# A delta-rule attention and a routed mixture of experts on one core: one sort product a chunk, narrower state and w products, earlier masks, two idle products

## The chip, the cores and the metric

The kernel runs on one core of one Trainium2 chip. The metric is device time in microseconds of one execution; before the change the median of three runs is 519.18 us (518.67 to 519.23). A further execution was taken with the hardware profiler; all lines of traces below come from it. Names of engines in its lines: PE is TensorE (PEld its weight loads), DVE is VectorE, ACT is ScalarE, POOL is GpSimd, SPq the queue of SyncE, which issues the DMAs.

## The reference

Two blocks, one after the other, in float32:

```python
# attention: batch 4, heads 8, 768 positions, head size 48
for t in range(S):
    y[:, :, t] = q[:, :, t] @ state                       # per batch and head
    v_old = state^T k_n[:, :, t]                          # k_n = k / (|k| + 1e-6)
    state += beta_t * outer(k_n[:, :, t], v_t - v_old)
x = y.transpose(0, 2, 1, 3).reshape(3072, 384)
# experts: 4 groups of 4, hidden size 1024
g_idx = argmax(x @ w_group); e_idx = argmax(x @ w_expert[g_idx])
out[token] = softmax_g * softmax_e * (relu(x @ w1[g, e]) @ w2[g, e])
```

Each of the 3072 tokens goes to one of 16 experts.

## The kernel before

**Attention in chunks.** The 768 positions are cut into 24 chunks (`NCH`) of 32 (`C`). The partitions hold 4 batches times 32 positions; a "quad" is the 32 partitions of one batch, a "pair" 64 partitions of two. Within a chunk the recurrence becomes a triangular system. `gram` (L251) makes the products of keys with keys and queries with keys; ScalarE copies them out (`gt`, `gq`). `inverse(g)` solves the triangular systems of four chunks at once (a group; six groups, `RG` = 4) on VectorE by about 95 small operations (L279 to L377), and transposes the result into `mt`. `spread` (L386, L388) copies `mt` into `mtb`, once for each parity of the batch and multiplied by 0 or 1 (`parity`), so that a 64x64 weight block for two batches has zeros off its diagonal. `mask(u)` (L268) does the same for the query products of chunk u, with the causal mask (`upper`), into `gqm`. `scale(u)` (L403) makes `vh`, the values of chunk u times the key norms.

**One chunk on TensorE.** `advance(u)` has four steps: (1) `a_ps` = `vh` (L416, an identity product) plus keys times state `s_bd` (L422), copied with the sign turned to `f` (ScalarE, L426), and queries times state into `o_ps` (L431); (2) `w_ps` = inverse times `f` (L439, by pairs), copied to `w` (L442); (3) the state product `s_ps` += keys times `w` (L449), its diagonal blocks copied to `s_bd` by ScalarE in two instructions (L455); (4) `o_ps` += masked queries times `w`, by pairs while later grams are made (L463), by quads in the last `LEAD` = 10 chunks (L468), copied to `x` (L472). Each product is recorded as two load and two matmul records.

**Routing and sorting.** `logits(u)` turns `x` round (L490), multiplies it by the router weights (L500). `route(r)` works for a group of four chunks (the last four chunks are two groups of two): choices, the place of each token within its expert (`place`), the weight (`what`), and per chunk a selection matrix `at` (L561, `turn_to`), which has a one where a token's place equals a column from 0 to 255 (`T` = 2 tiles of 128 columns). Two products per chunk (L621), one for each tile, add the tokens' row numbers and weights into `sorted_in`, which shares the first bank of `s_ps` with the state: columns 384 to 479. Groups 0 to 3 are "early" and do much of it on GpSimd; group 4 (chunks 16 to 19) and the last two on VectorE.

**The order.** All engines run in an order written out by hand (`manual_schedule`). The loop over chunks calls the steps; between them `work(n)` lets the tasks behind (an inverse, a route) issue VectorE instructions as far as their due allows (`due` grows by n * 180 times a rate, `SHARE` = 0.64 for an inverse), and `allow(...)` releases tasks held at a name. At the end of chunk u's turn come `mask(u + 1)` and `scale(u + 2)`, and then the loads of later chunks:

```python
work(12)
if u + 1 < NCH:
    mask(u + 1)
if u + 2 < NCH:
    scale(u + 2)
```

Ahead of the loop stand twelve grams, the first inverse, and the first step of chunk 0; the grams borrow the banks of `s_ps`, which is only later the state.

**Experts.** After the sort, each of the 16 experts takes up to 256 sorted tokens: `hidden` (L964), `second` (L983), weights loaded two experts ahead by SyncE's queue, tokens gathered and scattered by GpSimd.

Of the kernel before, what the change touches and what calls it, by code (L numbers as in the profile page):

```python
# [8 lines left out]
F32 = mybir.dt.float32  # L9
I32 = mybir.dt.int32  # L10
AX = mybir.AxisListType
ALU = mybir.AluOpType
# [3 lines left out]
C = 32  # L16
# [11 lines left out]
def constants(n_tokens, seq, n_experts, n_group, n_batch):  # L28
# [11 lines left out]
                                 .reshape(C, 2 * C) for b in range(n_batch)], axis=0),  # L40
        "tiny": np.full((128, 1), 1e-36),
# [25 lines left out]
def deltanet_then_moe(  # L67
# [109 lines left out]
    with ExitStack() as first:  # L177
# [10 lines left out]
        NB, NV = LEAD + 2, 3  # L188
        kqt_ = [ap_.tile([128, 2, NP, 128], F32, name=f"kqt{i}") for i in range(NB)]
# [74 lines left out]
        def mask(u):  # L264

            like = [128, H, 2, C]
            gqs[u] = wk.tile(like, F32, tag="gqm", name=f"gqm{u}", bufs=3)
            nc.vector.tensor_tensor(  # L268
                gqs[u], raws.pop(u)[:, :, None, :].to_broadcast(like),
                cut["upper"].rearrange("p (a t) -> p a t", a=2)[:, None].to_broadcast(like),  # L270
                op=ALU.mult)

        def inverse(g):
# [104 lines left out]
            mtb = wk.tile([128, RG * H, 2, C], F32, tag="mtb", name=f"mtb{g}")  # L378
            yield C * C
            turned_over.add(g)  # L380

            def spread(uu, a):
                rows = slice(uu * H, (uu + 1) * H)
                from_, by = mt.rearrange("p i r -> p r i")[:, rows], cut["parity"][:, a:a + 1]
                if g == uu == a == 0:
                    nc.vector.tensor_scalar(mtb[:, rows, a], from_, by, None, op0=ALU.mult)  # L386
                else:
                    nc.scalar.activation(mtb[:, rows, a], from_, ACT.Copy, scale=by)  # L388

            yield ACT_STEP  # L390
            for a in range(2):
                spread(0, a)
            mts[g] = mtb
            for uu in range(1, RG):
                for a in range(2):
                    yield SPREAD
                    spread(uu, a)
# [12 lines left out]
        def advance(u):  # L410
# [26 lines left out]
            for h in range(H):  # L437
                for b in pairs:
                    nc.tensor.matmul(w_ps[b, h], lhsT=mt[b, uu * H + (h % 2) * NP + h // 2],  # L439
                                     rhs=f[b, h], start=True, stop=True, skip_group_check=True)  # L440
# [5 lines left out]
            if u < NCH - 1:  # L446
                for j in range(NP):
                    for b in range(B):
                        nc.tensor.matmul(s_at[:, b, j], lhsT=k[quads[b], j],  # L449
# [9 lines left out]
            for h in range(H):  # L459
# [6 lines left out]
                else:  # L466
                    for b in range(B):
                        nc.tensor.matmul(o_ps[quads[b], h], lhsT=gq[quads[b], hq, b % 2],  # L468
# [36 lines left out]
        def route(r):  # L505
# [50 lines left out]
            mine = small("mine", [3, NE])  # L556
            like = [128, n, 3, NE]
            def turn_to(u):
# [3 lines left out]
                    at.rearrange("p t i -> p (t i)"), cut["places"], place[:, u:u + 1], None,  # L562
# [35 lines left out]
            if not final:  # L598
                nc.vector.tensor_reduce(place[:, u0:u0 + n], rk, axis=AX.X, op=ALU.add)
                yield  # L600
            nc.vector.reciprocal(what[:, u0:u0 + n, 2:3], cw)
            yield
            cs = slice(2 if not early and final else 0, 3)
            like[2] = cs.stop - cs.start
            (nc.gpsimd if early else nc.vector).tensor_tensor(
                mine[:, :, cs], hotf[:, :, None, :].to_broadcast(like),
                what[:, u0:u0 + n, cs, None].to_broadcast(like), op=ALU.mult)
# [5 lines left out]
            for g, u in enumerate(us):  # L613
# [5 lines left out]
                yield SORT  # L619
                for t in range(T):  # L620
# [65 lines left out]
        with tc.manual_schedule(engines={mybir.EngineType.PE, mybir.EngineType.DVE,  # L686
# [23 lines left out]
            for u in range(2 * RG, LEAD):  # L710
                gram(u, homes[u % len(homes)])
            start(inverse(1), 0.95)
# [55 lines left out]
            for u in range(NCH + 1):  # L768
# [3 lines left out]
                turned = logits(u - 1) if u else iter([None] * 2)  # L772
                if u:
# [55 lines left out]
                if u + 1 < NCH:  # L829
                    mask(u + 1)  # L830
# [366 lines left out]
```

## Time and profile before

| | us |
|---|---|
| median of three runs | 519.18 |
| the profiled execution | 511.25 |
| its span, first to last instruction | 509.0 |
| TensorE busy, of the span | 470.6 |
| VectorE busy | 250.3 |
| ScalarE busy | 188.9 |
| GpSimd busy | 193.7 |
| first w product starts | 42.49 |
| last w product (chunk 23) starts | 225.33 |
| first expert product starts | 238.95 |

The span is cut into stages: up to 42 us the first inverse, to 238 us the chunks with routing behind them, then the experts. A line of the chain of waits says when a piece of work began, how long it held the chain, and the engine, tile and line. A line of the timeline has start, duration, engine, line, operation, output and inputs, shapes. A record count behind x counts half products, as each is recorded twice.

### The profile page before, as it was taken

To read this page: it belongs to the slowest core of one execution; us is meant where nothing else is said; L and a number is where in the kernel's file an instruction comes from. 1 tells how busy PE (TensorE), PEld (TensorE's weight loads), DVE (VectorE), ACT (ScalarE), POOL (GpSimd) and SP (SyncE) were. 2 spreads that over 40 slices of the span, in tenths; PEclk is the share of its full clock that TensorE was granted. 3 is DMA by queue.
4 is the path that set the end of the run, shared out by engine and by line. 5 is a ranking of instruction groups with operands and counts; after the bars stand their busy time and mean duration, and the time that the engine had idled before them with its cause. 6 is when DMAs were issued, how large, how long until landed. Compare 5 with 4: busy or idle time off the path is not lost.

```text
span 509.0 us, 18246 instructions
## 1 busy us (share of the span) xinstructions
PE 470.6 (92%) x7844; PEld 437.8 (86%) x7844; DVE 250.3 (49%) x829; ACT 188.9 (37%) x397; POOL 193.7 (38%) x288
## 2 busy tenths in 40 slices
PE   4346999999999999999999999999999999999993
PEld 3235878888888888889999999999999999999992
DVE  3999999999999995527312012102201121011110
ACT  3224768687676767652111111111111211111110
POOL 0040200633806425010445564466435654355231
PEclk9999999999999999999999999999999999999997
DMA  5781434444423546210798788769868978879740
GB/s 178 246 311 40 153 135 157 160 154 158 134 71 117 160 147 198 74 45 17 180 370 249 250 268 269 228 220 331 269 193 282 321 270 260 262 253 310 256 134 26
DMA packets 57333, 99.94 MB, mean 196 GB/s; under 512 B 18974, under 2 KB 41433, under 8 KB 57251
## 3 DMA queue, kind: packets, MB, share of 16 engines
q1 hardware_dynamic: 51331, 88.76, 52.7%
q0 software_dynamic: 5920, 10.00, 6.4%
q8 instruction: 63, 1.03, 0.8%
q14 instruction: 19, 0.16, 0.1%
HBM read 84.61 MB, written 14.27 MB: 194 GB/s over the span
## 4 chain that ended last, share of the span: by engine, by line
PE 57%; DMA 20%; DVE 7%; ACT 5%; SPq 4%; issue 4%; POOL 2%; DVEq 0%; POOLq 0%; ACTq 0%
PE y_ps L983 12%; PE h_ps L964 12%; DMA y_dram<-yq 9%; DMA out_dram<-yo,to_i 5%; PE w_ps L439 5%; PE s_ps L449 5%; DMA yr<-y_dram 5%; PE a_ps L422 3%; SPq L1023 3%; PE l_ps L500 3%; ACT s_bd L455 3%; PE o_ps L463 3%; PE o_ps L431 3%; PE g_ps L251 2%; PE a_ps L416 2%
## 5 line engine op out<-in xcount | busy, mean ns | idle before, releaser
L983 PE MATMUL y_ps<-hid,w 128*128 128x224 f32 (+15 forms) x768 | 132.2, 331 | 0.0
L983 PEld LDWEIGHTS y_ps<-hid,w 128*128 128x128 f32 x768 | 129.0, 190 | 0.3
L964 PE MATMUL h_ps<-xt,w 128*128 128x232 f32 (+14 forms) x720 | 122.7, 330 | 0.0
L964 PEld LDWEIGHTS h_ps<-xt,w 128*128 128x128 f32 x720 | 120.1, 190 | 0.3
L936 POOL DMA_INDIRECT xq<-x_dram,from_q x92 | 87.6, 952 | 36.5 <-issue 24.1
L986 DVE COPY yt<-y_ps 128x232 f32<-128x232 f32 (+13 forms) x14 | 5.1, 366 | 139.7 <-PE y_ps L983 139.7
L967 ACT ACTIVATE hid<-h_ps 128x448 f32<-128x448 f32 (+15 forms) x64 | 32.1, 502 | 100.2 <-PE h_ps L964 100.2
L995 POOL DMA_INDIRECT out_dram<-yo,to_i x32 | 34.1, 1066 | 91.5 <-DVE yo L1033 80.0
L988 ACT ACTIVATE yt<-y_ps 128x224 f32<-128x224 f32 (+15 forms) x34 | 11.5, 337 | 116.6 <-PE y_ps L983 116.6
L360 DVE TENSOR_TENSOR t<-m 128x81 f32<-128x81 f32 (+13 forms) x156 | 51.8, 332 | 0.2
L366 DVE TENSOR_TENSOR m<-m,t 128x81 f32<-128x81 f32 (+13 forms) x156 | 51.4, 330 | 0.0
L455 ACT ACTIVATE s_bd<-s_ps 48x768 f32<-48x768 f32 x46 | 37.0, 805 | 13.9 <-PE s_ps L449 13.3
L343 DVE SCALAR_TENSOR_TENSOR m<-m 128x29 f32<-128x29 f32 (+27 forms) x174 | 40.7, 237 | 0.4
L388 ACT ACTIVATE mtb<-mt,con 128x256 f32<-128x256 f32 x47 | 34.2, 741 | 1.6 <-DVE mt L377 1.5
L1033 DVE TENSOR_SCALAR yo<-yr,gate 128x384 f32<-128x384 f32 (+14 forms) x28 | 11.1, 416 | 43.0 <-DMA yr<-y_dram 35.4
L439 PE MATMUL w_ps<-f,mtb 64*64 64x48 f32 x768 | 28.0, 224 | 3.9 <-DVE mtb L386 3.9
L251 PE MATMUL g_ps<-kqt 48*32 48x64 f32 (+1 forms) x1216 | 18.5, 241 | 13.5 <-issue 8.8
L439 PEld LDWEIGHTS w_ps<-f,mtb 64*64 64x64 f32 x768 | 25.1, 138 | 6.2 <-ACT mtb L388 4.1
L422 PEld LDWEIGHTS a_ps<-s_bd,kqt 128*32 128x32 f32 x736 | 15.3, 111 | 15.5 <-ACT s_bd L455 7.3
L539 POOL TENSOR_TENSOR acc<-acc,hots 128x16 f32<-128x16 f32 x16 | 5.7, 354 | 60.1 <-DVE hots L537 59.1
L251 PEld LDWEIGHTS g_ps<-kqt 48*32 48x32 f32 x1216 | 14.6, 118 | 15.3 <-issue 10.5
L449 PE MATMUL s_ps<-w,kv 32*128 32x96 f32 x736 | 27.4, 286 | 0.1
(159 smaller groups left out, 603.5 us busy)
## 6 DMA issues: line engine op xcount, KB each, us to landing
w<-in_w_dram SPq DMA_DIRECT2D x29, 1536.0 KB
kv<-in_kv_dram SPq DMA_DIRECT2D x24, 448.0 KB, 4.1
kqt<-in_kq_dram SPq DMA_DIRECT2D x20, 512.0 KB, 4.2
x_dram<-x SPq DMA_DIRECT2D x24, 192.0 KB, 2.3
w<-in_w_dram SPq DMA_DIRECT2D x24, 128.0 KB, 3.7
y_dram<-yq SPq DMA_DIRECT2D x36, 84.0 KB, 9.2
yr<-y_dram SPq DMA_DIRECT2D x14, 192.0 KB, 2.5
kqt<-in_kq_dram SPq DMA_DIRECT2D x8, 256.0 KB, 3.5
```

The costliest lines, as they stand in the source:

```text
L251: nc.tensor.matmul(g_out[quads[b], hh * NP + j, of], lhsT=kqt[rows, 0, j, quads[b]], rhs=kqt[rows, of, j, quads[b]], start=True, stop=True ...
L343: nc.vector.scalar_tensor_tensor(row, in0=m[:, j, 0:j], scalar=m[:, i, j:j + 1], in1=row, op0=ALU.mult, op1=ALU.add)
L360: nc.vector.tensor_tensor(tv, m[:, j + 2:, j:j + 1].to_broadcast([128, n, j]), m[:, j:j + 1, 0:j].to_broadcast([128, n, j]), op=ALU.mult)
L366: nc.vector.tensor_tensor(below, below, tv, op=ALU.add)
L388: nc.scalar.activation(mtb[:, rows, a], from_, ACT.Copy, scale=by)
L439: nc.tensor.matmul(w_ps[b, h], lhsT=mt[b, uu * H + (h % 2) * NP + h // 2], rhs=f[b, h], start=True, stop=True, skip_group_check=True)
L449: nc.tensor.matmul(s_at[:, b, j], lhsT=k[quads[b], j], rhs=w[quads[b], 2 * j:2 * j + 2], start=(u == 0 and j == 0), stop=True, skip_group_ ...
L455: nc.scalar.activation(s_bd[rows, :, :, hh, :], s_at[rows, :, :, hh * D:(hh + 1) * D], ACT.Copy)
L936: nc.gpsimd.indirect_dma_start(out=xq[:, g, :], out_offset=None, in_=x_dram[:, :].rearrange("n (q c) -> (n q) c", q=4), in_offset=bass.Ind ...
L964: nc.tensor.matmul(h_ps[:, k], lhsT=w1[:, j, (f + k) * 128:(f + k + 1) * 128], rhs=xt[:, j, 0:R], start=(j == 0), stop=(j == DC - 1), skip ...
L983: nc.tensor.matmul(y_ps, lhsT=w2[:, f, j * 128:(j + 1) * 128], rhs=hid[:, f], start=(f == 0), stop=(f == FC - 1))
L995: put = nc.gpsimd.indirect_dma_start(out=out[:, :], out_offset=bass.IndirectOffsetOnAxis(ap=to[0:P, i:i + 1], axis=0), in_=yo[0:P, :], in_ ...
```

## The change

- **State product.** Keys of a pair of heads lie in 128 columns, of which the last 16 are padding; 112 columns (`KR`) are loaded, and 112 rows of `s_ps` written.
- **Sort.** For chunks 0 to 19 (`one`) `at` has 128 columns only, from the place less 128 where it is 128 or more (`low`). What tells the two tiles apart moves to the other operand: `half` is one for the tile that a token is in, `what2` is `what` times `half` for both tiles, `mine` has 96 columns in place of 48. One product with 96 columns takes the place of two with 48.
- **Late masks.** From chunk 14 (`LATE`) on `mask` writes 256 elements a partition, with a mask of its own (`causal`, 32 more columns of constants), for the quads that L468 reads.
- **Last w.** For the last group (`SMALL`, chunks 20 to 23) `spread` makes one copy in place of two, without the multiplication, and w is made by quads, 32x32.
- **Order.** `mask(u + 1)` is called at the start of chunk u's turn, not at its end (chunk 0 excepted).
- **Idle products.** Two products of the identity with 384 columns of `below` into the first bank of `s_ps`, after the last gram ahead of the loop; nobody reads their values. They begin the bank's accumulation on all 128 rows.

```diff
@@ -38,6 +38,7 @@
     out = {
         "upper": np.concatenate([np.where(np.arange(2)[None, :, None] == b % 2, (i < k)[:, None], 0)
                                  .reshape(C, 2 * C) for b in range(n_batch)], axis=0),
+        "causal": np.tile(i < k, (n_batch, 1)),
         "tiny": np.full((128, 1), 1e-36),
         "eps": np.full((128, 1), 1e-6),
         "parity": np.stack([p // C % 2 == b2 for b2 in range(2)], axis=1),
@@ -186,6 +187,7 @@
         s_ps = pst.tile([128, B, 512], F32, tag="state", name="s_ps")
         s_at = s_ps[:, :, 0:H * D].rearrange("p b (j d) -> p b j d", j=NP)
         NB, NV = LEAD + 2, 3
+        LATE, SMALL, KR = NCH - LEAD, NGR - 1, 64 + D
         kqt_ = [ap_.tile([128, 2, NP, 128], F32, name=f"kqt{i}") for i in range(NB)]
         kv_ = [ap_.tile([128, H * (64 + D)], F32, name=f"kv{i}") for i in range(NV)]
 
@@ -264,7 +266,14 @@
         def mask(u):
 
             like = [128, H, 2, C]
-            gqs[u] = wk.tile(like, F32, tag="gqm", name=f"gqm{u}", bufs=3)
+            gqm = wk.tile(like, F32, tag="gqm", name=f"gqm{u}", bufs=3)
+            if u >= LATE:
+                gqs[u] = gqm.rearrange("p h a t -> p (h a t)")[:, 0:H * C].rearrange(
+                    "p (h t) -> p h t", t=C)
+                nc.vector.tensor_tensor(gqs[u], raws.pop(u), cut["causal"][:, None, :].to_broadcast(
+                    [128, H, C]), op=ALU.mult)
+                return
+            gqs[u] = gqm
             nc.vector.tensor_tensor(
                 gqs[u], raws.pop(u)[:, :, None, :].to_broadcast(like),
                 cut["upper"].rearrange("p (a t) -> p a t", a=2)[:, None].to_broadcast(like),
@@ -376,23 +385,28 @@
             mt = wk.tile([128, C, RG * H], F32, tag="mt", name=f"mt{g}", bufs=1)
             nc.vector.transpose(out=mt.rearrange("p i r -> p (i r)"), in_=flat)
             mtb = wk.tile([128, RG * H, 2, C], F32, tag="mtb", name=f"mtb{g}")
+            one_each = mtb.rearrange("p r a t -> p (r a t)")[:, 0:RG * H * C].rearrange(
+                "p (r t) -> p r t", t=C)
             yield C * C
             turned_over.add(g)
 
             def spread(uu, a):
                 rows = slice(uu * H, (uu + 1) * H)
                 from_, by = mt.rearrange("p i r -> p r i")[:, rows], cut["parity"][:, a:a + 1]
-                if g == uu == a == 0:
+                if g >= SMALL:
+                    nc.scalar.activation(one_each[:, rows], from_, ACT.Copy)
+                elif g == uu == a == 0:
                     nc.vector.tensor_scalar(mtb[:, rows, a], from_, by, None, op0=ALU.mult)
                 else:
                     nc.scalar.activation(mtb[:, rows, a], from_, ACT.Copy, scale=by)
 
+            halves = range(1 if g >= SMALL else 2)
             yield ACT_STEP
-            for a in range(2):
+            for a in halves:
                 spread(0, a)
-            mts[g] = mtb
+            mts[g] = one_each if g >= SMALL else mtb
             for uu in range(1, RG):
-                for a in range(2):
+                for a in halves:
                     yield SPREAD
                     spread(uu, a)
 
@@ -435,7 +449,7 @@
             mt = mts[g]
             w_ps = ps.tile([128, H, D], F32, tag="s", name=f"w_ps{u}")
             for h in range(H):
-                for b in pairs:
+                for b in quads if g >= SMALL else pairs:
                     nc.tensor.matmul(w_ps[b, h], lhsT=mt[b, uu * H + (h % 2) * NP + h // 2],
                                      rhs=f[b, h], start=True, stop=True, skip_group_check=True)
             w = wk.tile([128, H, D], F32, tag="w", name=f"w{u}")
@@ -446,7 +460,7 @@
             if u < NCH - 1:
                 for j in range(NP):
                     for b in range(B):
-                        nc.tensor.matmul(s_at[:, b, j], lhsT=k[quads[b], j],
+                        nc.tensor.matmul(s_at[0:KR, b, j], lhsT=k[quads[b], j, 0:KR],
                                          rhs=w[quads[b], 2 * j:2 * j + 2],
                                          start=(u == 0 and j == 0), stop=True,
                                          skip_group_check=True)
@@ -465,7 +479,7 @@
                                          skip_group_check=True)
                 else:
                     for b in range(B):
-                        nc.tensor.matmul(o_ps[quads[b], h], lhsT=gq[quads[b], hq, b % 2],
+                        nc.tensor.matmul(o_ps[quads[b], h], lhsT=gq[quads[b], hq],
                                          rhs=w[quads[b], h], start=False, stop=True,
                                          skip_group_check=True)
             x = wk.tile([128, DM], F32, tag="x", name=f"x{u}", bufs=4)
@@ -553,13 +567,19 @@
                 nc.scalar.activation(rk, r_ps, ACT.Copy)
             nc.scalar.activation(sx, sx, ACT.Exp)
             sums, ed, cw = small("sums", [L5]), small("ed", [G]), small("cw", [1])
-            mine = small("mine", [3, NE])
+            one = u0 < near[0]
+            mine = small("mine", [T * 3 if one else 3, NE])
             like = [128, n, 3, NE]
+            if one:
+                half, low, what2 = small("half", [T]), small("low", []), small("what2", [T, 3])
+                like[2] = T * 3
             def turn_to(u):
 
                 at = wk.tile([128, T, TILE], F32, tag="at", name=f"at{u}", bufs=6)
                 (nc.gpsimd if early else nc.vector).tensor_scalar(
-                    at.rearrange("p t i -> p (t i)"), cut["places"], place[:, u:u + 1], None,
+                    at[:, 0] if one else at.rearrange("p t i -> p (t i)"),
+                    cut["places"][:, 0:TILE] if one else cut["places"],
+                    low[:, u - u0:u - u0 + 1] if one else place[:, u:u + 1], None,
                     op0=ALU.is_equal)
                 ats[u] = at
 
@@ -598,13 +618,32 @@
             if not final:
                 nc.vector.tensor_reduce(place[:, u0:u0 + n], rk, axis=AX.X, op=ALU.add)
                 yield
+            if one:
+                at_u = place[:, u0:u0 + n]
+                nc.vector.tensor_scalar(half[:, :, 0], at_u, float(TILE), None, op0=ALU.is_lt)
+                nc.vector.tensor_scalar(half[:, :, 1], at_u, float(TILE), None, op0=ALU.is_ge)
+                yield
+                nc.vector.scalar_tensor_tensor(low, in0=half[:, :, 1], scalar=-float(TILE),
+                                               in1=at_u, op0=ALU.mult, op1=ALU.add)
+                yield
             nc.vector.reciprocal(what[:, u0:u0 + n, 2:3], cw)
             yield
+            if one:
+                to_both = [128, n, T, 3]
+                (nc.gpsimd if early else nc.vector).tensor_tensor(
+                    what2, what[:, u0:u0 + n, None, :].to_broadcast(to_both),
+                    half[:, :, :, None].to_broadcast(to_both), op=ALU.mult)
             cs = slice(2 if not early and final else 0, 3)
-            like[2] = cs.stop - cs.start
-            (nc.gpsimd if early else nc.vector).tensor_tensor(
-                mine[:, :, cs], hotf[:, :, None, :].to_broadcast(like),
-                what[:, u0:u0 + n, cs, None].to_broadcast(like), op=ALU.mult)
+            if one:
+                (nc.gpsimd if early else nc.vector).tensor_tensor(
+                    mine, hotf[:, :, None, :].to_broadcast(like),
+                    what2.rearrange("p n t c -> p n (t c)")[:, :, :, None].to_broadcast(like),
+                    op=ALU.mult)
+            else:
+                like[2] = cs.stop - cs.start
+                nc.vector.tensor_tensor(
+                    mine[:, :, cs], hotf[:, :, None, :].to_broadcast(like),
+                    what[:, u0:u0 + n, cs, None].to_broadcast(like), op=ALU.mult)
             if early:
                 yield SOON
             elif not final:
@@ -617,6 +656,13 @@
                 if r < NGR - 2 and u == u0:
                     yield NEXT
                 yield SORT
+                if one:
+                    nc.tensor.matmul(sorted_in["at"], lhsT=at[:, 0],
+                                     rhs=mine[:, g].rearrange("p c e -> p (c e)"),
+                                     start=not sorted_in["begun"], stop=True,
+                                     skip_group_check=True)
+                    sorted_in["begun"] = True
+                    continue
                 for t in range(T):
                     nc.tensor.matmul(sorted_in["at"][:, t * 3 * NE:(t + 1) * 3 * NE],
                                      lhsT=at[:, t], rhs=mine[:, g].rearrange("p c e -> p (c e)"),
@@ -709,6 +755,9 @@
             next(ahead)
             for u in range(2 * RG, LEAD):
                 gram(u, homes[u % len(homes)])
+            for n in (H * D, H * D):
+                nc.tensor.matmul(s_ps[:, 0, 0:n], lhsT=ident, rhs=cut["below"][:, 0:n],
+                                 start=True, stop=True, skip_group_check=True)
             start(inverse(1), 0.95)
             made = 0
             while 0 not in mts:
@@ -770,6 +819,8 @@
                     add_gathered(gathered, [0])
                 step = advance(u) if u < NCH else iter([None] * 4)
                 turned = logits(u - 1) if u else iter([None] * 2)
+                if 0 < u < NCH - 1:
+                    mask(u + 1)
                 if u:
                     next(step)
                 else:
@@ -826,8 +877,8 @@
                 if u % RG == RG - 3 and u // RG + 2 < NGR:
                     start(inverse(u // RG + 2), SHARE)
                 work(12)
-                if u + 1 < NCH:
-                    mask(u + 1)
+                if u == 0:
+                    mask(1)
                 if u + 2 < NCH:
                     scale(u + 2)
                 if u + NB < NCH:
```

## The prediction

> **What bounds the kernel now.** I read three stages first (columns: stretch in us, its length, then busy us of each engine with its instruction count, clock, DMA share, GB/s), then the page's slices.
>
> ```profile
> 42.00:197.00 155.00, 152.01 (x4429) 129.23 (x4433) 152.71 (x546) 108.02 (x209) 54.91 (x120) 1.00 0.42 137
> 197.00:238.00 41.00, 39.66 (x958) 34.84 (x955) 17.06 (x74) 24.12 (x51) 6.29 (x7) 1.00 0.23 75
> 238.00:509.00 271.00, 262.39 (x1569) 261.11 (x1568) 47.90 (x98) 43.94 (x99) 125.89 (x141) 0.99 0.75 244
> ...
> DVE  3999999999999995527312012102201121011110
> ```
>
> From 42 to 197 us TensorE (152.0 of 155) and VectorE (152.7 of 155) are both full. After 197 VectorE is half empty, and after 238 the experts keep TensorE full. No edit touches the experts, so the gain is how much sooner the attention ends.
>
> Which of the two full engines has the last word? The chain of waits names TensorE and ScalarE. One late chunk (17) of it: start, us, what.
>
> ```profile
> 177.31 0.87 PE a_ps L422 x32
> 178.18 0.66 PE o_ps L431 x32
> 178.84 0.48 PE t_ps L490 x3
> 179.31 0.38 PE s_ps L621 x4
> 179.69 1.06 PE w_ps L439 x32
> 180.76 0.78 PE l_ps L500 x6
> 181.53 1.12 PE s_ps L449 x32
> 182.69 0.04 issue
> 182.74 0.81 ACT s_bd L455
> 183.57 0.81 ACT s_bd L455
> ```
>
> A period is 7.11 us. The sort (L621), w (L439) and state product (L449) stand on it, so what they lose the period loses, until something else arrives last. VectorE is nearly that something. The timeline shows what it owes TensorE:
>
> ```profile
> 174.48 0.54 DVE L403 TENSOR_TENSOR vh<-kv,normt 128x384 f32<-128x384 f32 x1
> 176.24 0.91 PE L416 MATMUL a_ps<-vh,con 128*128 128x384 f32 x2
> ...
> 193.79 1.25 DVE L377 STREAM_TRANSPOSE mt<-m 128x1024 f32<-128x1024 f32 x1
> 196.37 1.37 ACT L388 ACTIVATE mtb<-mt,con 128x256 f32<-128x256 f32 x2
> 197.64 1.63 ACT L455 ACTIVATE s_bd<-s_ps 48x768 f32<-48x768 f32 x2
> ```
>
> The vh of chunk 17 ends at 175.02 and is read at 176.24: 1.2 us to spare. The last inverse is transposed by 195.04, ScalarE spreads it from 196.37. In this stage VectorE idles for about 1.5 us in all, in pieces of 0.25 us at most, none of them for TensorE. Its instructions stand in a fixed order, so each has a date that a faster TensorE cannot move.
>
> **What the Trainium skill says.** "TensorE: Matmul & The Clock Gate", section "LDWEIGHTS (loading the stationary operand)": the time goes with the columns, P/1.2 ns, not the rows. The trace agrees: 128 columns 192 ns (L449), 64 columns 138 (L439), 32 columns 105 (L468); 54 ns for 64 columns is 0.84 ns a column. The same page, Part 1: an idle array runs at half clock, and about 3.4 us of sustained work release it. The trace agrees on the halves (L416 x2 takes 1.65 us at 49.91, 0.91 at 58.50) but not on the time: TensorE works from 42.49 almost without a gap and is fast only from about 52. The same page's "Architectural detail" says that VectorE and ScalarE queues are strict FIFO, which the fixed dates rest on.
>
> **The change, part by part.**
>
> *State product, 112 columns for 128.* It is bound by loads: 32 records in 1.08 us, 34 ns each, four row groups side by side. Sixteen columns less are 13 ns of a load, a quarter of that per record, 3.3 x 32 = 0.11 us; in proportion (1/8 of 1.08) 0.135. I take 0.12 a chunk, for 23 chunks. No 112-column load is in the trace: nothing gained is the lower end unless an odd width breaks the overlap (a rival below).
>
> *Sort, one product for two.* 4 records become 2 of the same load and twice the columns (96). Twelve records took 1.37 us from start to the next w (216.31 to 217.68), 0.114 each, eight 1.0, 0.12 each: 0.24 saved for each of 20 chunks. It is paid by small VectorE operations (two halves, low), five times: 128x4 operations of 0.17 us, each 0.085 to 0.2 of VectorE's time, depending on whether it waits for its forerunner: 0.3 to 0.5. In groups 1 and 2 the reciprocal waited 0.24 for GpSimd, which covers half. To chunk 19 I count 0.5 + 0.2 + 0.2 = 0.9 us.
> GpSimd: four factors (at) per group fall from 1.0 to about 0.5 each, mine doubles (0.6 to about 1.1), what2 is new (0.3 to 1.0, as cw shows). The first at of a group comes 0.1 to 1.0 later; that of group 3 is ready at 198.44 and needed at 201.1. After a shift of 1.9 us 0 to 0.8 is left. I count nothing; the other end is 0.3 us.
>
> *Late masks halved.* Spacing to the next instruction is 602 ns for 512 elements and 468 for 384 (vh): 1.05 ns an element, so 256 save 0.27. Masks 14 to 16 lie ahead of vh(17): 0.8. Ahead of the last inverse there were masks to 18, five whole ones (3.0); then masks to 19, six halves (2.0): 1.0 saved.
>
> *Masks half a period sooner.* In VectorE's order mask(u+1) goes ahead of chunk u's inverse work; it waits only for copies made ten chunks earlier and for a buffer read three chunks before. Mask(16) ended at 174.5, 0.9 us before its reader; it gets a period more. vh(u+2) has the same work ahead of it. Cost 0: without the move mask(16) would be the next wait, at a gain over 0.9.
>
> *Last w by 32x32.* 32x32 products stand in the trace: L468, 64 records in 0.81 us (212.58 to 213.39), against 1.06 for 64x64. 0.25 for each of four chunks. The spreads fall from two to one a chunk: 0.74 us of ScalarE each.
>
> *Two idle products.* Two like L416 cold, 3.3 us, from the last gram (ends 38.6) to 41.9; the first w waits for VectorE's spread until 42.46. Cover 0.5 us. If they release the clock, chunk 0 to 1 shortens: 42.49 to 53.80 is 11.3 against a warm 7.55, up to 3.7 us. From below: nothing. `causal` adds 16 KB to the first constants, under 0.1 us at the 178 GB/s of that slice.
>
> **The sum.** TensorE alone would be, at chunk 17, 16 x 0.12 + 9 x 0.24 = 4.1 us ahead (7.8 with the clock). It can't be: vh(17) is there at 175.02 - 0.8 + 0.9 = 175.1, 0.1 for the semaphore, 175.2 against 176.24: gain **1.05**. The clock's 3.7 us are therefore lost whatever happens, and the sort and state savings before chunk 17 too. Chunks 17 and 18 add 0.36 each: 1.8 at chunk 19, and 2.2 when its state product ends. There the spread of the last inverse, ahead of s_bd on ScalarE, waits for 195.04 - 1.0 + 0.9 = 194.9; one spread of 0.74 gives 195.7, against 197.64: gain **1.9**. After it VectorE is out of the way.
> Chunk 20: sort 0.24, w 0.25, of which ScalarE's second spread takes back 0.13, state 0.12: 0.48. Chunk 21: two sorts 0.48, w 0.25, state 0.12: 0.85. Chunk 22: 12 and 8 records halved 1.2, w 0.25, state 0.12: 1.58. Chunk 23: none, its w copy waits behind two ScalarE products (L742). Together **2.9**.
> 1.9 + 2.9 = 4.8 us. The profiled execution took 511.25 us (span 509.0), so it becomes 506.4; the median of the runs lies 7.9 above it, and the same 4.8 taken from 519.18 gives **514.4**. A measurement of this kernel tells about 0.2% (1 us) from no change.
>
> **Rivals.**
> *A, the sum above*, VectorE's dates decide: 513.4 to 515.4, chance 0.60.
> *B, the new small work lands on the dates:* halves and low cost 0.5 in every group (0.6 more by chunk 17), what2 and mine stall the sorts of chunk 20, the loads of 112 gain nothing. 4.8 - 0.6 - 0.3 - 0.4 = 3.5, to 1.5 if stalls repeat: 515.4 to 518. For it: 1.2 us of margin at chunk 17; GpSimd's cw takes 1.0 us for four elements. Chance 0.17.
> *C, VectorE yields:* its dates move with TensorE. Then 3.7 + 22 x 0.12 + 12 x 0.24 + 2.9 = 12.1, 507.1; halfway 511. Against it: hardly any idle time on VectorE. Chance 0.13, most of it near 512.
> *D, slower:* 112 columns are no multiple of 32, and loads of the four row groups no longer overlap. Each record is then 34 ns plus what is lost; it decides from 4.8 / (23 x 32) = 6.5 ns a record on. Without any overlap a load is spaced like L500's, 0.78 / 6 = 130 ns: 32 x 96 = 3.1 us a chunk, some 70 us slower, 585. For it: no such width in the trace; against: time goes with columns, smoothly, at 32, 64 and 128. Chance 0.06.
> *E, nothing measurable* (stalls eat all but 1 us): 0.04.
>
> **How the numbers follow.** Faster is A, B and C: 0.90; same 0.04; slower 0.06. The range takes A, B to 516.8 (0.12) and C down to 512.2 (0.08): 0.80.
>
> **What would show it.** L449's loads near 178 ns and its 32 records near 0.95 us; L621 with half the records; L439 of the last four chunks near 0.81. VectorE still full to about 196, its last mt within 0.5 us of 195.0: the decisive line. A wait of a_ps L416 for vh near chunk 17, and of the spread for mt at chunk 19, both absent before. Products near 42 us in half the time, and yet no gain from it later. Expert stage unchanged at 271 us. Wrong if mt(5) ends much sooner, if o_ps waits for gqm, or if L621 waits for at.

## The result, and the profile after

The changed kernel took 511.44 us (median of four, 510.37 to 514.39), the kernel before 518.92 (four, 517.76 to 519.23; three of the four are those that the forecast started from): a ratio of 0.9869, with a 95% interval from 0.9825 to 0.9913, that is 4.5 to 9.1 us. The forecast was 4.8 us and 514.4, with a range from 512.2; the time lies 0.8 us below that range.

Later samples, with more executions of the same two kernels, give a smaller gain:

| sample | chip | changed | before | ratio (95%) | gain, us |
|---|---|---|---|---|---|
| on record, 4 and 4 executions | not recorded | 511.44 | 518.92 | 0.9869 (0.9825 to 0.9913) | 6.8 |
| e4, 22 and 65 | 12 | 509.03 | 512.69 | 0.9939 (0.9915 to 0.9963) | 3.1 |
| e9, 15 and 50 | 0 | 510.22 | 512.59 | 0.9945 (0.9920 to 0.9969) | 2.8 |

The medians are over all executions, while the ratios, and the gains taken from them, are estimated without the few slow ones, so that they aren't the quotients of the medians. So 4.8 us lies between them, and two things need explaining: why the base moves so much, and why the better samples stop at 3.

The profiled execution of the changed kernel took 511.43 us, span 509.7. That is no less than the profiled one of before (511.25), which stood 7.9 us under the median of the timed ones. Stages and VectorE's slices, as before:

```profile
42.00:197.00 155.00, 148.59 (x4410) 123.80 (x4409) 153.12 (x559) 108.33 (x210) 51.73 (x123) 0.99 0.43 138
197.00:238.00 41.00, 38.24 (x1067) 32.80 (x1063) 16.54 (x80) 21.42 (x46) 5.59 (x8) 1.00 0.23 73
238.00:509.00 271.00, 262.08 (x1565) 260.48 (x1563) 47.90 (x98) 43.94 (x99) 126.16 (x141) 0.99 0.75 244
...
DVE  2999999999999995427212012011211121101110
```

To 197 us TensorE is now busy 148.6 us, 3.4 less, and VectorE 153.1, as full as it was. The chain of waits, the turn of chunk 17 (7.11 us before):

```profile
177.95 0.87 PE a_ps L436 x32
178.82 0.66 PE o_ps L445 x32
179.48 0.48 PE t_ps L504 x3
179.96 0.20 PE s_ps L660 x2
180.15 1.06 PE w_ps L453 x32
181.22 0.78 PE l_ps L514 x6
181.99 1.01 PE s_ps L463 x32
183.09 0.81 ACT s_bd L469
183.92 0.81 ACT s_bd L469
```

From 177.95 to the next a_ps at 184.78 it is 6.83, which is 0.28 less: the sort gave 0.18 and the state product 0.11, where the forecast had 0.36 for both. VectorE's dates in the same execution:

```profile
175.04 0.55 DVE L417 TENSOR_TENSOR vh<-kv,normt 128x384 f32<-128x384 f32 x1
176.88 0.91 PE L430 MATMUL a_ps<-vh,con 128*128 128x384 f32 x2
...
193.96 1.25 DVE L386 STREAM_TRANSPOSE mt<-m 128x1024 f32<-128x1024 f32 x1
```

The last inverse ends at 195.21 (195.04 before); the forecast was 194.9. But a_ps of chunk 17 starts 1.3 us after its vh, so it isn't this date that holds it here. One line of the waits tells of something new (waited for: us in total, times, longest), on GpSimd:

```profile
PE s_ps L660 <- POOL at L579: 2.4, 2, 1.8
```

and the timeline around the second of these waits shows what followed it:

```profile
164.75 0.46 PE L660 MATMUL s_ps<-mine,at 128*128 128x96 f32 x2 [0.66 <-POOL at L579]
...
166.98 1.82 PE L463 MATMUL s_ps<-w,kv 32*112 32x96 f32 x32
168.74 1.50 PE L482 MATMUL o_ps<-w,gqm 32*32 32x48 f32 x64
```

The last two products take 1.04 and 0.88 us elsewhere. The record of the clock has one stretch of half speed here, from 167.0 to 170.4. Later, in chunks 20 to 22, TensorE stood idle for 1.1 us that no engine explains ("issue"), 0.9 of it in one piece; the first trace of the kernel before has none there:

```profile
PE o_ps L482 <- issue: 0.9, 1, 0.9
```

### The profile page after: what moved, and what is told of

Its sections match the earlier page's. It is cut to its first block, busy times and chain, and to the rows that moved or that the text cites. A ratio compares the mean times of both kernels' runs of the same rounds, so it can differ in the third digit from the quotient of the medians.

```text
span 509.7 us, 18443 instructions
## 1 busy us (share of the span) xinstructions
PE 468.0 (92%) x7936; PEld 430.9 (85%) x7936; DVE 249.9 (49%) x845; ACT 186.5 (37%) x393; POOL 190.1 (37%) x292
## 3 DMA queue, kind: packets, MB, share of 16 engines
q8 instruction: 64, 1.05, 0.8%
## 4 chain that ended last, share of the span: by engine, by line
PE 54%; DVE 20%; DMA 11%; POOL 5%; issue 4%; ACT 3%; SPq 1%; DVEq 0%; POOLq 0%; ACTq 0%
PE y_ps L1034 18%; PE h_ps L1015 18%; DMA out_dram<-yo,to_i 5%; DVE t L369 5%; DVE m L375 4%; DMA y_dram<-yq 3%; DVE m L352 3%; PE w_ps L453 3%; ACT s_bd L469 3%; PE s_ps L463 3%; PE l_ps L514 2%; DMA yr<-y_dram 2%; PE a_ps L436 2%; PE o_ps L445 2%; PE t_ps L504 1%
## 5 line engine op out<-in xcount | busy, mean ns | idle before, releaser
L352 DVE SCALAR_TENSOR_TENSOR m<-m 128x29 f32<-128x29 f32 (+27 forms) x174 | 41.8, 243 | 0.4
L453 PEld LDWEIGHTS w_ps<-f,mtb 64*64 64x64 f32 (+1 forms) x896 | 24.3, 128 | 5.7 <-issue 2.9
L453 PE MATMUL w_ps<-f,mtb 64*64 64x48 f32 (+1 forms) x896 | 27.8, 218 | 1.4 <-issue 1.1
L401 ACT ACTIVATE mtb<-mt,con 128x256 f32<-128x256 f32 x39 | 28.4, 742 | 0.7 <-DVE mt L386 0.7
L463 PE MATMUL s_ps<-w,kv 32*112 32x96 f32 x736 | 25.3, 273 | 0.3 <-issue 0.3
```

The source lines that it names most:

```text
L352: nc.vector.scalar_tensor_tensor(row, in0=m[:, j, 0:j], scalar=m[:, i, j:j + 1], in1=row, op0=ALU.mult, op1=ALU.add)
L463: nc.tensor.matmul(s_at[0:KR, b, j], lhsT=k[quads[b], j, 0:KR], rhs=w[quads[b], 2 * j:2 * j + 2], start=(u == 0 and j == 0), stop=True, sk ...
```

## The experiments

"Date" below is the time at which VectorE has something ready, in its fixed order. The two theories named in the expectations: VectorE's dates swallow whatever TensorE gains ahead of chunk 17 (theory 1), or the idle products and the clock make the difference (theory 2).

**The kernel before, once more (e0), and the idle products alone (e1) or left out (e2).** e1 adds these lines to the kernel before, and e2 takes them out of the changed one.

```diff
+            for n in (H * D, H * D):
+                nc.tensor.matmul(s_ps[:, 0, 0:n], lhsT=ident, rhs=cut["below"][:, 0:n],
+                                 start=True, stop=True, skip_group_check=True)
```

> The kernel before, unchanged, for a trace of a further execution. Theory 1 (VectorE's dates carry the whole difference): its trace looks like the first one, 511 us when profiled, full clock from about 52 us to the experts' end. Theory 2 (the array's half clock is in the executions that were timed): most executions take near 519 us, and the trace of such a one shows the half clock for some 16 us more than the first one did (8 us lost at half speed).

> The kernel before with only the two idle products added. Theory 1: no difference (within 1 us of 519), since what TensorE gains at the start is taken back at VectorE's dates. Theory 2: the idle products release the clock near 44 us, and most of the 7.5 us come from them: 511 to 514 us.

> The changed kernel without the two idle products. Theory 1: as the changed kernel, 511 to 512 us. Theory 2: back near the kernel before, 517 to 519 us.

Measured, all on chip 15: before 517.01 (42 executions) and again 517.19 (20); idle products alone 517.00, ratio 0.9992 (0.9965 to 1.0018); all but the idle products 512.83, 0.9894 (0.9826 to 0.9961), from four executions. The idle products give nothing that can be seen, and the rest of the change gives the gain.

The further trace of the kernel before (519.17 us) shows where its time goes. Everything to chunk 17 runs 1.6 us later (a_ps at 177.85 in place of 176.24). From a_ps of chunk 23 to the experts it is 20.8 us in place of 16.6: TensorE runs at half clock from 232.1 for 6.8 us, and ten products of L729 take longer. The first line is from the first trace, the second from e0:

```profile
231.33 2.14 PE L729 MATMUL x_ps<-at,x 128*128 128x224 f32 x10
235.33 3.89 PE L729 MATMUL x_ps<-at,x 128*128 128x224 f32 x10
```

The experts took 2 us more. Theory 2 foretold half clock in such a trace, but some 16 us of it, and from the idle products; it is 6.8 us, and with the idle products (e1) the end of the attention has such a stretch as well.

This goes with the chip. The later samples were taken on four chips, and the medians of the kernel before are 517.0 on chip 15, 517.8 on chip 5, 512.7 on chip 12 and 512.6 on chip 0. Every trace from chips 15 and 5, whichever the kernel (e0 to e3, e12 to e14), has 3.4 to 10.2 us of half clock at the end of the attention; none of the eight from chips 12 and 0 has. The first profile, with 511.25, is quicker than all 62 executions of the kernel before on chip 15 (514.33 at least) and has no such stretch, but lies within the range of chips 12 and 0 (from 510.1). On which chip it ran, and on which the first timings, isn't recorded; that the 7.9 us between them are two chips is likely and not shown. Each chip was sampled once, so that chip and time of the sample can't be told apart.

**Masks back at the end of the turn (e3).**

```diff
-                if 0 < u < NCH - 1:
-                    mask(u + 1)
...
-                if u == 0:
-                    mask(1)
+                if u + 1 < NCH:
+                    mask(u + 1)
```

> The changed kernel with every mask made at the end of the turn before its chunk, as the kernel before has it. By the prediction a mask then arrives last at some chunks in the middle (mask 16 had 0.9 us to spare), which costs 0 to 1.5 us: 511.5 to 513 us. If the clock decides (theory 2), it makes no difference beyond 1 us unless the waits let the clock fall.

Measured: 513.05, 0.9911 (0.9880 to 0.9941), against 512.83 for e2 in the same sample, which differs from e3 by the idle products too: no difference to see. One o product waited for its mask, 0.4 us. In exchange VectorE's dates came sooner: the inverse of group 1 ends at 70.16, against 70.83 in e2 (the first inverse at 41.56 and 41.54). One mask more stands ahead of every inverse in the changed order. And the waits for `at` are gone in e3.

**The changed kernel, in a larger sample (e4, e9).**

> The changed kernel again, in more executions and beside as many of the kernel before. Theory 1 (VectorE's dates, the sum of 4.8 us, seen from a slow or a quick sample): 4.5 to 6 us under the kernel before of the same sample. Theory 3 (the sum missed a gain of 2 to 3 us that every execution has): 7 us or more under it.

> The changed kernel beside the one before it in this list, on the same chip: 3 to 5 us under the kernel before.

Measured as in the table: 3.1 and 2.8 us. Theory 3 (2 to 3 us missed by the sum) is out, and both are below what theory 1 and the second expectation had. The trace of e4 is like that of the result: waits for `at` of 1.6 and 0.7 us, half clock from 167.4 to 170.9, a_ps of chunk 17 at 177.10 with its vh at 175.81. That of e9 has no half clock there:

```profile
175.07 0.88 PE L482 MATMUL o_ps<-w,gqm 32*32 32x48 f32 x64
175.09 0.54 DVE L417 TENSOR_TENSOR vh<-kv,normt 128x384 f32<-128x384 f32 x1
175.88 0.91 PE L430 MATMUL a_ps<-vh,con 128*128 128x384 f32 x2
```

Its vh is ready at 175.63, and TensorE comes to a_ps straight from the o products, without a recorded wait. Here the two engines arrive almost together.

The times of the changed kernel lie in two groups: 506.7 to 509.3 and from 510.6 on in e4, 506.6 to 508.5 and from 510.2 on in e9; those of the kernel before on the same chips have no such gap in their middle. The traces of e4 (508.69) and e9 (507.84) are from the quicker group, whose middle is some 5 us under the median of the kernel before. What the other half of the executions loses is in no trace from these chips.

**More work on VectorE (e5).** Twelve operations that nobody reads, one a turn, chunks 5 to 16.

```diff
+                if 4 < u < 17:
+                    more = wk.tile([128, 512], F32, tag="more", name=f"more{u}", bufs=1)
+                    nc.vector.tensor_tensor(more, cut["below"][:, 0:512], cut["below"][:, 512:1024],
+                                            op=ALU.mult)
```

> The changed kernel with one more VectorE operation of 512 elements (0.60 us) in each turn from chunk 5 to 16, twelve in all, 7.2 us, that nobody reads. Theory 1: VectorE's dates move by all of it: the last inverse is transposed near 202.5 us in place of 195.3, the a_ps product of chunk 17 starts near 183 in place of 176.1, the total grows by about 7 us (near 519). Rival C of the prediction (VectorE yields, TensorE and ScalarE alone set the period): 0 to 2 us.

Measured: 515.53 against 509.03 for e4 in the same sample, 6.5 us more by the medians and 5.7 by the ratios, for 7.2 us of work. The timeline of e5:

```profile
181.58 0.54 DVE L417 TENSOR_TENSOR vh<-kv,normt 128x384 f32<-128x384 f32 x1
183.60 0.91 PE L430 MATMUL a_ps<-vh,con 128*128 128x384 f32 x2
...
201.24 1.25 DVE L386 STREAM_TRANSPOSE mt<-m 128x1024 f32<-128x1024 f32 x1
```

a_ps of chunk 17 moved by 6.5 us against e4 and the last inverse by 7. Rival C, a VectorE that yields, is out: most of the added work passes into the total. It doesn't pass by the date of chunk 17, though: a_ps starts 1.5 us after its vh here. TensorE had lost its time earlier, by a wait of 3.5 us for `at` at 133, which stands on GpSimd behind work that waits for VectorE, and by half clock from 135.7 to 149.3.

**vh by GpSimd (e6).**

```diff
-            nc.vector.tensor_tensor(
+            (nc.gpsimd if u > 2 else nc.vector).tensor_tensor(
                 vh.rearrange("p (j f) d -> p f j d", f=2),
...
```

> The changed kernel with vh made by GpSimd from chunk 3 on: 0.47 us a chunk, some 7 us by chunk 17, off VectorE. Theory 1: the last inverse ends 6 to 8 us sooner, TensorE is free at chunk 17 and 19, and the savings that were lost ahead of chunk 17 come through: 2 to 4 us under the changed kernel, if GpSimd (some 1 us for each) is not late itself. Rival C: within 1 us of the changed kernel.

Measured: 512.60, 3.6 us over e4; a miss. The last inverse ended at 197.23, later, not sooner. The timeline shows the greater part of the reason:

```profile
111.76 0.35 DVE L375 TENSOR_TENSOR m<-m,t 128x200 f32<-128x200 f32 x1
111.87 0.93 POOL L417 TENSOR_TENSOR vh<-kv,normt 128x384 f32<-128x384 f32 x1 [2.38 <-PE a_ps L436]
112.03 1.00 DVE L369 TENSOR_TENSOR t<-m 128x209 f32<-128x209 f32 x1
```

A VectorE operation that takes 0.36 us takes 1.00 while GpSimd's runs. Taken over 42 to 197 us, VectorE's operations beside the 18 vh on GpSimd took 6 to 7 us more than the same ones beside nothing, depending on how overlaps are counted; about 8.5 us had been saved. VectorE also waited 1.4 us for square roots that GpSimd finished late; the rest isn't accounted for. GpSimd's vh came late too, 3.5 us at chunk 7, behind the square roots. The Trainium skill has the contention in "SBUF — State Buffer", section "Who interferes with whom": a VectorE instruction with two SBUF inputs contends with a GpSimd one that reads SBUF, since its second input comes through a read interface that the two share. The run agrees with that (1.00 for 0.36). Since VectorE lost most of what it was spared, the run can't tell theory 1 from rival C.

**Parts alone: sort (e7), state product (e10), late masks and w (e11).** Each is that part's lines of the diff, in the kernel before.

> The kernel before with only one sort product a chunk for chunks 0 to 19. By the prediction's terms: VectorE has 0.5 to 0.9 us more ahead of chunk 17 and no saving there, so 0.2 to 0.6 us are gained at chunk 17, 0.24 more at each of chunks 17 to 19 and 1.9 us in chunks 20 to 22: 2.5 to 3 us under the kernel before. If the wait for at that the trace of the changed kernel shows (1.8 us at chunk 12) matters for the end, 0 to 1.5 us.

> The kernel before with only the 112-column state product. By the prediction: 32 records in 0.95 to 0.97 us in place of 1.08; 0.12 us a chunk, of which what is saved ahead of chunk 17 up to 1.2 us counts, and then 0.12 for each of six chunks: 1.5 to 1.9 us under the kernel before. If it is lost elsewhere: 0 to 1 us.

> The kernel before with only the halved late masks and the 32x32 products for w of the last four chunks. By the prediction: nothing from the masks while TensorE sets the period (VectorE only gets 0.8 us more to spare at chunk 17), 0.25 us for each of chunks 20 to 22 less 0.13: 0.5 to 0.7 us under the kernel before.

| part alone | ratio (95%) | gain, us | forecast |
|---|---|---|---|
| sort | 0.9948 (0.9925 to 0.9971) | 2.7 | 2.5 to 3 |
| state | 0.9968 (0.9948 to 0.9987) | 1.6 | 1.5 to 1.9 |
| masks and w | 0.9994 (0.9973 to 1.0015) | 0.3 | 0.5 to 0.7 |
| idle products (e1) | 0.9992 (0.9965 to 1.0018) | 0.4 | 0 |

Each interval holds what was forecast for the part, and the sort and the state product give a gain that is clear of noise. From the first to the last inverse VectorE takes 154.07 us in the kernel before, 155.02 with the sort alone (0.9 forecast), 152.61 with the halved masks, and 153.97 with the whole change (0.1 less forecast). Alone they come to 5.0 us; together the kernel has 3. With intervals of 1.0 to 1.4 us to either side of each, and three chips, the difference is not clear of noise.

**The selection matrices sooner (e8).** The fourth `at` of an early group stood on GpSimd behind the inverse's square roots, which wait for VectorE.

```diff
             if early:
                 yield SOON
-            elif not final:
+            if not final:
                 for u in us:
                     turn_to(u)
             for g, u in enumerate(us):
-                if early:
-                    turn_to(u)
                 at = ats[u]
```

> The changed kernel, with the four selection matrices (at) of an early group made one after the other as soon as its places are known, so that the fourth no longer stands behind the inverse's square roots on GpSimd. If the waits of the sort at chunks 11 and 15 (1.6 to 1.8 and 0.7 us) and the half-clock window behind the second (some 1.2 us) take away gain: both waits and the window near 167 us are gone, the a_ps product of chunk 17 starts at VectorE's date (near 176.0 in place of 177.1), and the total is 1 to 2 us under the changed kernel. If these waits only fill time that VectorE's dates take anyway: within 0.5 us of it.

Measured: 510.45, 0.9939 (0.9914 to 0.9964), and 510.22 for the changed kernel beside it. Both waits for `at` and the half clock near 167 are gone, and what takes their place are waits on VectorE's dates, that for the vh of chunk 17 among them, which the prediction had named. The waits of e8, from 160 to 200 us:

```profile
PE a_ps L436 <- ACT s_bd L469: 2.0, 5, 1.3
PE a_ps L430 <- DVE vh L417: 1.1, 2, 0.8
```

TensorE stood ready for chunk 16 at 166.3 (it began that chunk at 168.78 in e9, at 168.95 before) and waited 0.3 us for vh, waited 1.3 us for a state copied behind the spread of the inverse of group 4, and 0.8 us for the vh of chunk 17, which it started at 175.73. Of 2.2 us that had been won against e9 on TensorE, 0.15 were left ten microseconds later. The spread of the last inverse waited for VectorE as well, 0.3 us. Here, and in no trace of the changed kernel, VectorE's dates are seen to hold TensorE at the places that the prediction named. By chunk 20 it is 0.7 us ahead of e9 again, and loses that to 1.1 us of issue in chunks 20 to 22; the total is the same (0.9939 and 0.9945 of the kernel before).

**Work taken off VectorE (e12), with w narrower as well (e13), without the idle products (e14).** All three stand on e8. In e12 every mask from chunk 1 is halved, and the o products that read them are 32x32 in place of 64x64; e13 sets SMALL to 1 too, so that w is 32x32 from group 1; e14 is e12 without the idle products.

```diff
-        LATE, SMALL, KR = NCH - LEAD, NGR - 1, 64 + D
+        LATE, SMALL, KR = 1, NGR - 1, 64 + D
-                if u + LEAD < NCH:
+                if u < LATE:
```

> The changed kernel with the selection matrices made sooner, and with half masks and 32x32 o products from chunk 1 on in place of chunk 14. VectorE loses 0.27 us for each of 13 masks, 3.5 us; TensorE 0.25 for each of 13 chunks. VectorE's dates: the last inverse ends near 191.7 in place of 195.2, and the total falls by 2.5 to 3.5 us against the changed kernel (5.5 to 7 us under the kernel before). If TensorE and ScalarE set the period: also up to 3 us, but with the last inverse still waiting for nobody and a_ps of chunk 17 more than 1 us after its vh. If more TensorE instructions (64 more a chunk) cost as much as they save: no change.

> As the run before it, and w by 32x32 products with single spreads from group 1 on. No work of VectorE is taken away: if its dates decide, within 1 us of the run before it, although TensorE has 0.25 us and ScalarE 0.74 us less a chunk. If TensorE sets the period there: 2 to 3 us less.

> As the run before the last, without the two idle products. If VectorE's dates decide, within 1 us of it; if the idle products' 1.5 to 3.7 us at the start count now that VectorE is lighter, 1 to 3 us more.

Measured, on chip 5 and against 517.75: 517.26, 1.0004 (0.9971 to 1.0037); 532.67, 1.0274 (1.0226 to 1.0322); 518.39, 0.9993 (0.9968 to 1.0018). e12 has no gain over the kernel before, and w by 32x32 from group 1 costs 15 us on top of it (532.67 - 517.26, 14 by the ratios). The changed kernel itself wasn't run on this chip, so what it gains there isn't known. VectorE did get lighter: 152.64 us from first to last inverse, and vh of chunk 17 stood ready at 174.00 while a_ps came at 177.51. Now TensorE was late. Its waits from 42 to 190 us in e12:

```profile
PE o_ps L482 <- issue: 3.2, 4, 1.6
PE g_ps L253 <- issue: 2.1, 3, 1.5
```

"Issue" is idle time that no other engine explains; it falls in the middle of runs of small products. Half clock came four times by 230 us, three of them within the chunks, 3.4 us each.

Where these pauses lie can be counted in the traces. Number TensorE's instructions (loads, matmuls, waits) from the start and look at pauses in its matmuls of more than 0.2 us, from 46 to 240 us, that the profile puts down to issue. The 17 traces have 83. Of these, 73 come at the same place in a block of 256 instructions (the 192nd to 197th), and the other ten all lie in the w products of chunk 23. The 73 come to 1.0 us in the first trace of the kernel before (2 pauses), 2.9 in that of the result (5), 4.7 in e12 (7), 6.8 in e14 (11) and 15.1 in e13 (17; its trace is 3.6 us over its median). In e13 that is as much as was lost. This reads as instructions that arrive at TensorE 256 at a time and sometimes late; the place is shown by the count, the reason isn't.

So the third possibility in the expectation for e12 fits what happened: more instructions cost what they save. Those for e13, at most 3 us of gain or none, were missed by far. Theory 1 holds, by this, only while TensorE has few enough instructions.

## Why the prediction was right or wrong

**Right: VectorE's dates.** They stood near where the sum put them: last inverse 194.9 forecast, 195.2 measured; 154 us from first to last inverse with and without the change; 7.2 us put on VectorE cost some 6 (e5). That they take back what TensorE wins is seen in e8. In the changed kernel itself it isn't: the two signs that the prediction named, a wait of a_ps for vh near chunk 17 and of the spread for mt at chunk 19, are in none of its traces (result, e4, e9), and its a_ps of chunk 17 starts 1.3, 1.3 and 0.25 us after its vh.

**Right: the parts.** "The clock's 3.7 us are therefore lost whatever happens": e1 gives 0.4 (-0.9 to 1.8). The late part, 2.9 us from chunk 20 to 23: in e9 that stretch takes 21.41 us in place of 24.25, 2.84 less, and in e4 2.83; in the trace of the result, with its 1.1 us of issue, 1.5. The loads of 112 columns take 177 ns (178 forecast), w by 32x32 0.82 us from its start to the next product (0.81).

**Wrong: the last step, "the same 4.8 taken from 519.18".** This is the step that failed. It took three executions for the base, and the sentence after it, that a measurement tells 1 us from no change, was too sure: the record's own interval is 2.3 us to either side. The kernel before has medians of 518.9, 517.0, 512.7, 512.6 and 517.8 in five samples, the last four on four chips. From 517.0 the same sum gives 512.2, from 512.7 it gives 507.9; the changed kernel took 511.4, 509.0 and 510.2. The range held the cases of the mechanism and nothing for the base. The first profile (511.25, 7.9 under the median) had shown that something outside the sum was at work, and the prediction carried the 7.9 along without a cause. That the record's interval of 4.5 to 9.1 us holds the 4.8 says little, as wide as it is.

**Too large: the terms ahead of chunk 20.** How far a trace is ahead of the first one of the kernel before, in us (e8 is the changed kernel with `at` sooner):

| trace | a_ps of chunk 17 | chunk 20 | chunk 23 | first expert product |
|---|---|---|---|---|
| forecast | 1.05 | 1.9 | 4.8 | 4.8 |
| result | -0.64 | 0.23 | 1.73 | 0.58 |
| e4 | -0.86 | 0.02 | 2.85 | 2.40 |
| e9 | 0.36 | 0.91 | 3.75 | 3.42 |
| e8 | 0.51 | 1.64 | 2.88 | 3.11 |

Chunk 17: vh came at 175.63 in e9, not 175.1; 0.4 of that is a later start of VectorE (first inverse at 41.35 against 40.96), which the second trace of the kernel before has as well (41.39), so it isn't the change's.
Chunks 17 to 19: 0.28 in an undisturbed turn in place of 0.36, because on the chain two sort records less save 0.18, not 0.24. I had taken the spacing within long runs of records; on the chain the first load is under way before the product ahead of it ends (179.00 and 179.28 in e9). In e9 the turn of chunk 17 saves nothing, since its queries-times-state product takes 0.3 us longer.
In the traces of the result and of e4 the waits for `at` and the half clock behind them make chunk 17 start 1.3 us after its date. Issue in chunks 20 to 23 then takes more from the result and from e8.

**Wrong: "Cost 0" for the masks half a period sooner.** One mask more stands ahead of every inverse, a halved one for the last two: 0.7 us on the dates of groups 1 to 3 and 0.4 on those of groups 4 and 5 (e2 against e3). With that `at` came late (in e3 the waits are gone), a wait that the prediction priced at 0 to 0.3 and placed at chunk 20, and whose coming it had named as a sign of being wrong. It was 1.6 to 1.8 us at chunk 11 and 0.7 at chunk 15, for the fourth matrix of a group, which stands behind the square roots; I had looked at the first ones only. Without these waits the total is the same (e8).

By size the larger samples fall into rival B (1.5 to 3.5 us, chance 0.17), and later dates and stalls of the sort are what it had, though at other chunks and beside causes that it didn't name: issue and half clock.

**Open:** why the chips differ, which chips the first timings and the first profile ran on, what makes the slower half of the changed kernel's executions, and how much of the record's 6.8 us is more than the scatter of four executions.

## What to carry to other kernels

When two engines are both full, follow what each owes the other as a list of dates: what is saved on one before the other's next date is lost if it arrives there first, as 2 us were between chunks 16 and 17 of e8. Price a gain against the scatter of the base, over executions and over chips, not against one profile; if profile and median differ by more than the gain, the range has to hold that difference. And narrower products mean more instructions, which have a price of their own: w by 32x32, forecast to gain in the last four chunks, cost some 15 us when used from the second group on.

## What the runs showed of the hardware

- **Half clock after short pauses.** A pause of 0.69 us in TensorE's work at 74.5 was followed by 3.4 us of half clock at 75.3 (e7), one of 0.66 at 164.1 by the stretch at 167.0 (the result), and within one of 3.5 from 97.7 half clock began at 100.8 (e6). But 1.77 us at 131.3 (the result) and 0.69 at 74.6 (e0) had no such stretch. "TensorE: Matmul & The Clock Gate", Part 1 (the clock gate), speaks of an idle window of 3.4 us; here stretches came behind far shorter pauses, sometimes. They are 3.4 us long or multiples of it (6.8, 10.2, 13.7), as its window has it. That the pause brings the stretch is read from the order of events, not shown by a run.
- **With the idle products the full clock came early in some executions only:** from 44.1 (the result) and 44.6 (e4), but from 55.1 in e1 and 53.8 in e5, although they ran at the same place. In e8 and e9 it came at 41.3 and 43.8, and fell back 3.4 us later to half, for 6.8 us.
- **Chips differ, and so does their clock.** The kernel before takes 517.0 and 517.8 us on two chips and 512.7 and 512.6 on two others, each sampled once. All seven traces from the first two have half clock at the end of the attention, none of the eight from the others.
- **TensorE's unexplained pauses lie 256 instructions apart, or a multiple:** 73 of 83 in 17 traces. With 32x32 in place of 64x64 for the o products and w (e13) they come to 15.1 us.
- **A GpSimd operation holds VectorE up** for a good part of its own length: 0.64 us for one vh of 0.93 (e6). Doubling `mine` made its part of this grow from 0.3 or 0.4 us for four to 2.0 for three between 42 and 197 us; halving `at` gave 0.9 back.
